# A linear attention followed by a Fourier mixing block: five output buffers, a smaller state mask, GpSimd operations one after the other, and a new order

## The chip, the cores and the metric

The kernel runs on one core of one Trainium2 chip. The metric is the time of one execution on the device, in microseconds (us), inputs and outputs in device memory. Five engines work side by side, each through its own queue in order: TensorE (PE in the profile: matmuls; PEld are its weight loads), VectorE (DVE), ScalarE (ACT), GpSimd (POOL) and SyncE (SP), which here issues DMAs only. ScalarE and GpSimd issue some DMAs too.

## The reference

Two blocks one behind the other. The first is a linear attention with a decaying state, over 4 batches, 8 heads, 768 steps and head size 48:

```python
for t in range(S):
    cur = np.einsum('bhd,bhe->bhde', u[None] * kt, vt)
    y[:, :, t] = np.einsum('bhd,bhde->bhe', rt, state + cur)
    state = w[None, :, :, None] * state + np.einsum('bhd,bhe->bhde', kt, vt)
```

The second takes the result as x (4 x 768 x 384), mixes it with the real part of a Fourier transform over both axes, normalizes, and adds an MLP of width 1536:

```python
X = np.fft.fft(np.fft.fft(x, axis=1), axis=2)
u = x + np.real(X)
un = (u - mean(u)) / np.sqrt(var(u) + 1e-06)
return u + np.maximum(un @ w_ch1, 0.0) @ w_ch2
```

## The kernel before

The sequence of a batch is cut into six chunks of 128 steps, 24 chunks in all. In a chunk k and r are scaled by powers of the decay (`KR`, line 386, with the tables `wtab`, lines 326 and 328, which ScalarE makes from `lw`, the logarithm of w), transposed (`tp` on TensorE at line 410, or a transposing DMA to `KRT`, line 416), multiplied with each other (`A`, line 444), masked (`MA`, on GpSimd at line 453 or VectorE at 456) and applied to v (`y`, line 535). The state is carried from chunk to chunk in `S` (line 490): the accumulated update is multiplied with a mask `WD` that is one, or the decay over three chunks, where a head's own block lies, and zero elsewhere. The result goes to `X` (line 543). Each batch is then folded by its symmetries (`EO`, `HH`, `XF`; the last is line 603, for the first batch 567), transformed over the sequence (`fp`, line 636) and over the width (`mp`, line 677), and gives the sum `UF` (line 689), scaled as `UB`, which is transposed to `UNT` on TensorE or by a DMA (line 747). The MLP takes half a batch at a time, eight halves of three blocks: `hp` (line 765, twelve groups of three matmuls), the relu `HT` (ScalarE at 770 or VectorE at 771), `mo` (line 786, four groups of three for each block), the epilogue `osb` (line 796, on VectorE) and the output DMA (line 799 from GpSimd, 800 from SyncE). `osb` h.j is block j of half h.

All operations are written down as a list of some 1,650 with names, alternatives (which engine does it, or nothing) and needs; the string `ORDER` is a list of their numbers with the alternative chosen, worked out by a planner beforehand. `emit` walks through it and issues each operation; an engine executes its operations in the order of this list. Many tiles live in rings of buffers; a new tile takes the buffer whose last user stands earliest in the list, and waits for that user. `osb` has a ring of three buffers. An operation waits for the data it needs, and for nothing else; two operations of GpSimd that share no data have no wait between them.

Matmuls on zeros (`idle`, line 272, of 512 columns, and line 366, of 384) can be put anywhere in the order; this one holds nine of the first kind and five of the second, all in the first 29 us.

The start (function `prelude`): ScalarE loads w, then a table set, computes `lw` (line 324), the six tables `wtab`, and after them `lwc` and `wdec` (lines 330 and 331), which need four small loads `wuc` that GpSimd issues (line 302). W1 comes in two halves and W2 in three parts, all issued by GpSimd (lines 840 and 843).

Of the kernel before, what the change touches and what calls it, by code (L numbers as in the profile page):

```python
# [61 lines left out]
class _Schedule:  # L62
# [12 lines left out]
    def emit(self, order):  # L75
        last = {}
# [5 lines left out]
        for k, (n, a) in enumerate(order):  # L82
# [7 lines left out]
            fn = o["alts"][a][2]  # L90
            if fn is not None:
                fn()
# [78 lines left out]
def kernel(  # L171
# [110 lines left out]
    def prelude():  # L282
# [30 lines left out]
        for i in range(2):  # L313
            op(("WD0", i), [("DVE", "msWD", lambda i=i: nc.vector.memset(WD[i], 0.0)),
                            ("POOL", "msWD", lambda i=i: nc.gpsimd.memset(WD[i], 0.0))], w=[("WD0", i)])
            one(("XF0", i), "DVE", "msXF", lambda i=i: nc.vector.memset(XFs[i][:, :, :, 4 * CH:], 0.0))
# [565 lines left out]
```

## Time and profile before

| | us |
|---|---|
| median of 3 runs | 182.74 |
| lowest and highest run | 179.83, 183.57 |
| profiled execution, span from the first to the last instruction | 180.9 |
| TensorE busy (share of the span) | 161.1 (89%) |
| VectorE | 133.4 (74%) |
| ScalarE | 109.8 (61%) |
| GpSimd | 84.1 (46%) |

The profiled execution gives its span alone, which lies 1.8 us under the median and inside the runs. Busy time is the time in which an engine executes something of the program; a busy TensorE may run at either of two clocks, and the granted clock is given as a share of the full one. Waits are put down to what ended them. A DMA's time to landing runs from its issue to the signal that its data have arrived.

### The profile page before, as it was taken

What the parts mean: (1) busy time and instruction counts of PE and PEld (TensorE: products, weight loads), DVE (VectorE), ACT (ScalarE), POOL (GpSimd) and SP (SyncE); (2) the same over time, 40 slices, a digit from 0 to 9 for tenths busy, and PEclk for the clock granted to TensorE, in tenths of its full rate; (3) what the DMA queues carried; (4) which work ended last, traced back from release to release, by engine and by line L of the source; (5) the groups of instructions that cost most, each with busy time, mean ns of one, the idle gap of its engine ahead of it and who ended that gap; (6) DMA issues with size and microseconds to landing.
All of it is one profiled execution on the core that took longest, in us unless ns stands there. A gap on an engine that the chain in (4) does not pass through costs nothing.

```text
span 180.9 us, 4262 instructions
## 1 busy us (share of the span) xinstructions
PE 161.1 (89%) x1595; PEld 112.7 (62%) x1595; DVE 133.4 (74%) x311; ACT 109.8 (61%) x264; POOL 84.1 (46%) x118
## 2 busy tenths in 40 slices
PE   6229987899799999999469999999999999999992
PEld 1126654887666766786236677756776866666661
DVE  5478899999699897999254688979859846542621
ACT  2366977398878987877332647888390553621430
POOL 6344857775563707498524233927783133101000
PEclk9999999699999999999957999999999999999999
DMA  6999999999488999969999995569510203711212
GB/s 125 202 219 211 242 203 201 225 183 198 76 151 178 156 210 184 243 150 180 137 264 224 213 203 119 145 127 210 114 35 2 80 11 65 196 49 43 87 43 87
DMA packets 98118, 27.08 MB, mean 150 GB/s; under 512 B 94369, under 2 KB 96930, under 8 KB 98098
## 3 DMA queue, kind: packets, MB, share of 16 engines
q1 hardware_dynamic: 92912, 21.70, 61.0%
q0 software_dynamic: 2064, 4.53, 11.4%
q10 hardware_dynamic: 3122, 0.59, 1.9%
q8 instruction: 12, 0.20, 0.5%
q14 instruction: 8, 0.07, 0.1%
HBM read 19.77 MB, written 4.72 MB: 135 GB/s over the span
## 4 chain that ended last, share of the span: by engine, by line
PE 72%; DVE 12%; DMA 9%; ACT 2%; issue 2%; SPq 1%; DVEq 0%; ACTq 0%
PE bank L765 27%; PE bank L786 25%; DMA out_dram<-osb 4%; PE bank L636 3%; PE bank L444 3%; PE bank L677 3%; DMA kr<-in_k_dram 3%; DVE KR L386 2%; DMA vt<-in_v_dram 2%; PE bank L410 2%; DVE MA L456 2%; PE bank L475 2%; PE bank L535 2%; DVE XF L567 2%; PE bank L514 1%
## 5 line engine op out<-in xcount | busy, mean ns | idle before, releaser
L765 PE MATMUL bank<-UNT,W 128*128 128x384 bf16 x288 | 56.5, 337 | 5.0 <-DVE osb L796 3.9
L786 PE MATMUL bank<-W,HT 128*128 128x384 bf16 x276 | 52.7, 326 | 0.0
L770 ACT ACTIVATE HT<-bank 128x384 bf16<-128x384 f32 x67 | 29.6, 497 | 31.7 <-PE bank L765 31.6
L765 PEld LDWEIGHTS <-W 128*128 128x128 bf16 x288 | 31.5, 116 | 19.5 <-issue 7.7
L786 PEld LDWEIGHTS <-HT 128*128 128x128 bf16 x276 | 25.9, 98 | 14.1
L453 POOL TENSOR_SCALAR_AFFINE_SELECT MA<-AC 128x512 bf16<-128x512 bf16 x26 | 17.1, 667 | 13.9 <-ACT AC L451 13.8
L796 DVE SCALAR_TENSOR_TENSOR osb<-bank,rstd,UF 128x384 f32<-128x384 f32 x23 | 14.1, 614 | 12.6 <-PE bank L786 8.1
L771 DVE TENSOR_SCALAR HT<-bank 128x384 bf16<-128x384 f32 x29 | 15.6, 551 | 8.4 <-PE bank L765 8.3
L386 POOL TENSOR_TENSOR KR<-kr,wtab 128x384 bf16<-128x384 f32 x17 | 17.3, 1030 | 5.7 <-ACT lwc L330 4.9
L410 PE MATMUL bank<-ident,KR 128*128 128x128 bf16 x112 | 12.5, 253 | 7.4 <-DVE KR L389 2.8
L386 DVE TENSOR_TENSOR KR<-kr,wtab 128x384 bf16<-128x384 f32 x25 | 16.4, 671 | 1.8 <-ACT wtab L326 1.8
L708 ACT ACTIVATE squares<-UF,sm 128x384 bf16<-128x384 f32 x24 | 14.8, 617 | 3.9 <-DVE UF L689 3.7
L451 ACT CAST AC<-bank 128x512 bf16<-128x512 f32 x26 | 14.8, 588 | 3.9 <-PE bank L444 2.1
L410 PEld LDWEIGHTS <-KR 128*128 128x128 bf16 x112 | 9.3, 114 | 11.5 <-DVE KR L386 4.1
L799 POOL DMA_DIRECT2D out_dram<-osb x11 | 6.3, 571 | 21.9 <-DVE osb L796 19.3
L456 DVE TENSOR_TENSOR MA<-bank,mtri 128x512 bf16<-128x512 f32 x22 | 14.7, 681 | 0.7 <-PE bank L444 0.6
L689 DVE SCALAR_TENSOR_TENSOR UF<-bank,X 128x384 f32<-128x384 f32 x21 | 11.1, 554 | 5.4 <-PE bank L677 4.7
L636 PE MATMUL bank<-te_t,XF 128*128 128x193 bf16 x108 | 13.0, 260 | 0.0
L523 DVE TENSOR_TENSOR TT<-V,bank 128x384 bf16<-128x384 bf16 x18 | 9.9, 547 | 2.2 <-ACT V L402 0.8
L636 PEld LDWEIGHTS <-XF 128*128 128x128 bf16 x120 | 10.8, 102 | 0.9
L644 ACT CAST TT<-bank 97x386 bf16<-97x386 f32 x13 | 7.1, 606 | 5.6 <-PE bank L636 5.5
L420 ACT COPY KRT<-bank 128x512 bf16<-128x512 bf16 x16 | 9.3, 592 | 1.5 <-PE bank L410 1.5
(109 smaller groups left out, 266.3 us busy)
## 6 DMA issues: line engine op xcount, KB each, us to landing
kr<-in_k_dram SPq DMA_DIRECT2D x23, 192.0 KB, 4.1
kr<-in_r_dram SPq DMA_DIRECT2D x23, 192.0 KB, 3.9
vt<-in_v_dram SPq DMA_DIRECT2D x23, 192.0 KB, 4.0
out_dram<-osb SPq DMA_DIRECT2D x12, 192.0 KB, 2.6
out_dram<-osb POOLq DMA_DIRECT2D x11, 192.0 KB, 3.3
W<-in_moe_w_ch_dram POOLq DMA_DIRECT2D x2, 576.0 KB, 9.0
W<-in_moe_w_ch_dram POOLq DMA_DIRECT2D x3, 384.0 KB, 6.4
te_t<-te_c SPq DMA_DIRECT2D x1, 579.0 KB, 5.7
```

What stands on the lines that cost most here:

```text
L386: eng.tensor_tensor(out=o, in0=x, in1=y, op=AluOp.mult)
L410: nc.tensor.transpose(tps[s]()[:, p, :], KR()[:, s, p, :], ident)
L451: op(("AC", i, a), [("ACT", "AC", lambda: nc.scalar.copy(AC(), A_ps[a]())), ("NONE", "", None)], r=[("A", i)], w=[("AC", i, a)], new=[AC], ...
L453: op(("MA", i, a), [("POOL", "MA", lambda: nc.gpsimd.affine_select(out=MA[a](), in_=AC(), pattern=[[0, NP], [1, 128]], base=0, channel_mul ...
L456: ("DVE", "MA", lambda: nc.vector.tensor_tensor(out=MA[a](), in0=A_ps[a](), in1=mtri.unsqueeze(1).to_broadcast([128, NP, 128]), op=AluOp.m ...
L636: nc.tensor.matmul(fp()[:, par, :], lhsT=lhsT[:, g * CH:g * CH + 128], rhs=rhs, start=(nb == 0 and par == 0), stop=(nb == last and par == ...
L708: ("ACT", "SQ", lambda: nc.scalar.activation(out=squares, in_=UF()[:, j, :], func=Act.Square, scale=-float(DM), bias=sm()[:, j:j + 1], acc ...
L765: nc.tensor.matmul(hp(), lhsT=W1[:, dt, ft // 4 * 512 + ft % 4:(ft // 4 + 1) * 512:4], rhs=UNT()[:, :, dt, :], start=(dt == 0), stop=(dt = ...
L770: op(("HT", hf, ft), [("ACT", "HT", lambda: nc.scalar.activation(out=HT()[:, ft, :], in_=hp(), func=Act.Relu, scale=-1.0)), ("DVE", "HT", ...
L771: ("DVE", "HT", lambda: nc.vector.tensor_scalar(out=HT()[:, ft, :], in0=hp(), scalar1=-1.0, scalar2=0.0, op0=AluOp.mult, op1=AluOp.max))],
L786: nc.tensor.matmul(mo(), lhsT=HT()[:, ft, j * 128:(j + 1) * 128], rhs=W2[:, ft, :], start=(ft == 0), stop=(ft == 11))
L796: one(("osb", hf, j), "DVE", "osb", lambda: nc.vector.scalar_tensor_tensor(out=osb(), in0=mo(), scalar=rstd()[:, j:j + 1], in1=UF()[:, j, ...
```

## The change

Four things change together.

1. `osb` has five buffers in its ring instead of three.
2. `WD`, the mask of the state, is kept as one number per row, pair and half (128 x 4 x 2) instead of being written out over the 48 columns; the state product reads it with a stride of zero. Its memsets and copies shrink with it.
3. `emit` adds a wait: every GpSimd operation that is not a DMA waits for the end of the GpSimd operation before it. After a DMA that GpSimd issues a nop is put in, and the next operation waits for that.
4. `ORDER` is new throughout: places, engines, and which tiles take which way. VectorE has 309 operations instead of 290, ScalarE 213 instead of 229 with its DMAs, GpSimd 122 instead of 114, TensorE 442 groups instead of 448. The nine zero matmuls of line 272 are left out; the five of line 366 stay. Two transposes on TensorE more stand for one transposing DMA less.

The diff, with the order cut to its ends:

```diff
-    def emit(self, order):
-        last = {}
+    def emit(self, tc, order):
+        nc, last, before = tc.nc, {}, None
...
-            fn = o["alts"][a][2]
-            if fn is not None:
-                fn()
+            eng, key, fn = o["alts"][a]
+            if fn is None:
+                continue
+            fn()
+            if eng != "POOL":
+                continue
+            if "dma" in key:
+                before = nc.gpsimd.nop().ins
+                continue
+            ins = next(i for i in reversed(nc.cur_bb.bb.instructions) if i.engine == mybir.EngineType.Pool)
+            if before is not None:
+                tc.add_manual_dep(ins, before.name, mybir.DependencyInfo(mybir.DependencyClass.Sync, mybir.DependencyReason.DATA),
+                                  reason="one after the other")
+            before = ins
...
 ORDER = """
-152 158 180.1 208 202 203 20 150 151 205 206 209 210 2 159 162 173 155 1 164 211 204 212 153 182 199.1 200.1 154 157
...
-1648.1 1652 1653 1654.1
+199 170.1 208 152 158 209 167.1 159 160 150 200 153 202 155 203 151 177 162 204 201.1 154 163 205 180.1 173 164 165
...
+1646 1647 1648.1
...
-    WD = [const([128, NP, 2, D], F32, f"WD{i}") for i in range(2)]
+    WD = [const([128, NP, 2], F32, f"WD{i}") for i in range(2)]
...
-    ring("osb", 3, [128, DM], F32)
+    ring("osb", 5, [128, DM], F32)
...
-            op(("WD0", i), [("DVE", "msWD", lambda i=i: nc.vector.memset(WD[i], 0.0)),
-                            ("POOL", "msWD", lambda i=i: nc.gpsimd.memset(WD[i], 0.0))], w=[("WD0", i)])
+            one(("WD0", i), "DVE", "tiny", lambda i=i: nc.vector.memset(WD[i], 0.0))
...
-            one(("WD", 0, a), "DVE", "ms192", lambda rows=rows, a=a: nc.vector.memset(WD[0][rows, :, a, :], 1.0), r=[("WD0", 0)])
-            one(("WD", 1, a), "DVE", "wdcopy", lambda rows=rows, a=a: nc.vector.tensor_copy(
-                WD[1][rows, :, a, :], wdec[rows, :].unsqueeze(2).to_broadcast([64, NP, D])), r=["wdec", ("WD0", 1)])
+            one(("WD", 0, a), "DVE", "tiny", lambda rows=rows, a=a: nc.vector.memset(WD[0][rows, :, a], 1.0), r=[("WD0", 0)])
+            one(("WD", 1, a), "DVE", "small", lambda rows=rows, a=a: nc.vector.tensor_copy(WD[1][rows, :, a], wdec[rows, :]),
+                r=["wdec", ("WD0", 1)])
...
-            op(("S", i + 1), [("DVE", "S", lambda: nc.vector.tensor_tensor(out=Sn(), in0=u_ps(), in1=d, op=AluOp.mult))]
+            op(("S", i + 1), [("DVE", "S", lambda: nc.vector.tensor_tensor(out=Sn(), in0=u_ps(), in1=d.unsqueeze(3).to_broadcast([128, NP, 2, D]), op=AluOp.mult))]
...
-        sch.emit(_order())
+        sch.emit(tc, _order())
```

Parts of the new order, read by their names, each in the sequence of its engine's queue:

```
GpSimd, start:   KR0.4 KR0.1 wuc.0.0 icol_i wuc.1.0 wuc.1.1 S0.2 wuc.0.1 ident ...
ScalarE, start:  load w, table set, load v of chunk 0, lwc, lw, six tables wtab, ...
GpSimd, end of the first batch's folds:  W1 (second half), HH 0.5.0, XF 0.5.0, MA 6.0, W1 (first half), KR 9.1, TR 0.0, ...
SyncE, batch 1:  KRT 16, KRT 17, UNT 1.0, k 19, r 19, output 0.1, UNT 1.1, v 17, KRT 14, ...
VectorE, batch 1:  MA 16.0, X 13, X 15, HT 2.7, HT 2.8, S 17, osb 1.2, HT 2.11, ...
TensorE, between the places of output 0.1 and osb 1.2:  hp 2.8, 2.5, 2.2, 2.11, 2.1, A 17, hp 2.6
```

In the old order GpSimd's outputs 0.1, 0.0, 1.1 and 0.2 stand among its arithmetic of batch 1, the output 1.1 right behind `TT` 15 and 16 places ahead of `osb` 1.2, which takes its buffer.

## Rows read from the trace of the kernel before

**Rows 1.** by stage (windows): stretch, busy us per engine (instructions), granted clock, DMA share, GB/s

```profile
13.10:47.90 34.80, 30.03 (x411) 22.96 (x411) 32.68 (x78) 27.14 (x65) 21.85 (x31) 0.95 1.04 203
47.90:70.00 22.10, 22.06 (x233) 15.27 (x234) 20.27 (x43) 18.75 (x46) 11.45 (x14) 1.00 0.88 160
...
84.00:90.00 6.00, 4.00 (x60) 2.81 (x58) 2.93 (x7) 3.19 (x8) 4.04 (x5) 1.00 1.17 143
90.00:98.00 8.00, 6.10 (x29) 3.21 (x29) 3.35 (x7) 1.64 (x4) 3.23 (x2) 0.57 1.09 244
98.00:177.60 79.60, 79.54 (x678) 55.54 (x676) 54.09 (x125) 43.44 (x111) 26.58 (x35) 1.00 0.45 104
```

**Rows 2.** VectorE's timeline: start us, us, line, operation, [idle before <- what ended it]

```profile
91.23 0.62 DVE L796 SCALAR_TENSOR_TENSOR osb<-bank,rstd,UF 128x384 f32<-128x384 f32 x1 [4.30 <-DMA out_dram<-osb]
```

**Rows 3.** chain that ended last, in order of time: start us, us, what

```profile
47.91 0.65 PE bank L765 x3
...
84.68 6.53 DMA out_dram<-osb
...
91.90 4.96 PE bank L765 x15
...
154.60 4.39 PE bank L765 x27
```

**Rows 4.** SyncE's DMA issues, 76 to 100 us (timeline, same columns)

```profile
78.12 4.05 SPq L416 DMA_TRANSPOSE KRT<-KR  x3
...
84.27 2.47 SPq L747 DMA_TRANSPOSE UNT<-UB  x1
```

**Rows 5.** by line: operation, tiles, shapes, count | busy us, mean ns | idle before

```profile
L523 DVE TENSOR_TENSOR TT<-V,bank 128x384 bf16<-128x384 bf16 x18 | 9.9, 547 | 2.2 <-ACT V L402 0.8 <-PE bank L508 0.7 <-ACT HT L770 0.7
...
L490 DVE TENSOR_TENSOR S<-bank,WD 128x384 bf16<-128x384 f32 x8 | 4.4, 548 | 0.0
...
L337 DVE COPY WD<-wdec 64x192 f32<-64x192 f32 x2 | 1.0, 484 | 0.0
...
L314 DVE MEMSET WD<- 128x384 f32 x2 | 0.8, 378 | 0.1
```

**Rows 6.** timeline of all engines, first 16 us

```profile
5.65 0.58 POOL L302 DMA_DIRECT2D wuc<-in_u_dram  x1
...
8.93 0.61 ACT L326 ACTIVATE wtab<-HT,ncol 128x384 f32<-128x384 f32 x1 [2.69 <-DMA kr<-in_k_dram]
...
10.96 0.19 ACT L330 ACTIVATE lwc<-wuc 128x4 f32<-128x4 f32 x1
```

**Rows 7.** DMA issues: tensors, queue, count, KB each, median us to landing

```profile
out_dram<-osb SPq DMA_DIRECT2D x12, 192.0 KB, 2.6
out_dram<-osb POOLq DMA_DIRECT2D x11, 192.0 KB, 3.3
W<-in_moe_w_ch_dram POOLq DMA_DIRECT2D x2, 576.0 KB, 9.0
...
wuc<-in_w_dram POOLq DMA_DIRECT2D x2, 0.8 KB, 4.2
```

**Rows 8.** GpSimd's timeline, 20 to 40 us

```profile
26.07 0.55 POOL L558 TENSOR_TENSOR HH<-X 128x192 bf16<-128x192 bf16 x1
26.58 0.56 POOL L567 TENSOR_TENSOR XF<-HH 128x196 bf16<-128x196 bf16 x1
...
33.77 1.39 POOL L558 TENSOR_TENSOR HH<-X 128x192 bf16<-128x192 bf16 x2
35.24 0.51 POOL L567 TENSOR_TENSOR XF<-HH 128x196 bf16<-128x196 bf16 x1
...
36.68 1.56 POOL L840 DMA_DIRECT2D W<-in_moe_w_ch_dram  x2
```

**Rows 9.** by line, the zero matmuls on TensorE

```profile
L272 PE MATMUL bank<-zero 128*128 128x512 bf16 x9 | 4.0, 512 | 1.5 <-DVE wuc L296 1.3 <-ACT KRT L420 0.2
...
L366 PE MATMUL bank<-zero 128*128 128x384 bf16 x5 | 1.8, 391 | 0.0
```

122 rows, old and new, of the table ORDER are left out of this document.

## The prediction

> **What bounds the kernel now.** I read four views: busy time by stage, the chain that ended last, the timeline of single engines, and the DMA issues. The stage table comes first [rows 1]. From 13.1 to 47.9 us VectorE (DVE) is busy 32.68 of 34.80 us: it prepares the first batch and sets the pace, and TensorE (PE) works beside it. From 47.9 us on, when the first matmul of the MLP starts, PE is busy 22.06 of 22.10, then 79.54 of 79.60 from 98 to 177.6. Those stretches are worth what their PE work is worth. In between lies the one hole: from 84 to 90 PE is busy 4.00 of 6.00, from 90 to 98 it is busy 6.10 of 8.00 at a mean granted clock of 0.57.
>
> The DVE timeline names the cause: the epilogue `osb` at 91.23 us waited 4.30 us for a DMA that was emptying its buffer [rows 2]. The chain shows the same, `out_dram<-osb` from 84.68 for 6.53 us, and behind it fifteen matmuls of L765 in 4.96 us, 0.331 each, where 27 of the same take 4.39 later, 0.163 each [rows 3]: PE came back at 1.2 instead of 2.4 GHz. That output had to wait on GpSimd's queue, and it travelled beside the transposing DMAs that SyncE issued from 78.12 and at 84.27 [rows 4]. By the rows the hole costs 2.00 + 1.90 idle and 6.10 x (1 - 0.57) = 2.6 of clock, 6.5 us in all.
>
> So the span reads: first MLP matmul at 47.9, then 177.6 - 47.9 = 129.7 us, of which 6.5 are the hole and 123.2 are PE work, then 3.3 us for the last epilogue and output: 47.9 + 123.2 + 6.5 + 3.3 = 180.9.
>
> **The change part by part.**
>
> *Five output buffers.* With three, `osb` 1.2 waits for the landing of output 1.1. With five, read off the new order by the same rule (the buffer whose last user stands earliest), it waits for output 0.1. That removes this wait, 6.5 us with its clock, if output 0.1 has landed. It is the third DMA on SyncE behind the transpose `UNT` 1.0, after k and r of chunk 19. Between its issue and `osb` 1.2 the new order puts six groups of three MLP matmuls on PE, 18 x 0.163 = 2.9 us. An output from SyncE lands after 2.6 us at the median [rows 7], at worst after the 6.53 of [rows 3]; so VectorE waits 0 to 3.6 us. PE has other banks to write meanwhile. I take 0.5 us of PE time and keep 0 to 3.6 (6.5 if the clock falls again, a rival below). `osb` 3.1 comes only 18 places after output 1.1, whose buffer it takes; VectorE is busy 54.09 of 79.60 us there [rows 1], and a wait of about 1 us hides in that idle time.
>
> *Mask as one number per row and head.* Two memsets of 378 ns become writes of a few numbers, and so do the two copies of 484 ns [rows 5]; 1.8 us in all, less some 0.3 for the short ones that stay. With the two memsets of ones beside them I take 1.8 off VectorE, all of it before the first MLP matmul. The state product now reads its second operand with stride zero. The product with a full operand takes 548 ns; the nearest row with a spread operand, `TT` at L523, takes 547 [rows 5]. I cost it at nothing; eight such products would have to grow by 60 ns each to cost half a microsecond.
>
> *The start.* In the new order ScalarE computes `lwc`, which needs all four small GpSimd loads `wuc`, before `lw` and the six tables of powers; in the old one it came after them, at 10.96 us [rows 6]. The last of the four was issued at 5.65 [rows 6]. It is now the eighth GpSimd operation, which I estimate at 4.3 us, and these loads land after 4.2 us [rows 7]: 8.5. `lw` and six tables follow, each about 0.5 apart, and the last table ends near 12.2. In the old order the tables were held as well, by ScalarE's own DMA issue, until 8.93, and ended at about 11 [rows 6]. So the late start of the first table is mostly absorbed: 0 to 1.1 us, and I take 0.8.
>
> *VectorE's queue.* Up to the last operation that the first MLP matmul needs, both orders put 95 operations on VectorE; the swaps are between operations of near length. The first batch therefore ends 0.8 - 1.8 = 1.0 us earlier for VectorE, at 46.9. But the second half of W1 is now issued behind three GpSimd operations that follow the last fold. The old order issued both halves from 36.68 [rows 8]; with the 0.8 of the start and one masking operation I put it at 38.2. These loads take 9.0 us to land [rows 7]: 47.2, and the third group of MLP matmuls needs them. I take 47.3 for the start of steady PE work, from 46.2 (only VectorE counts) to 48.5 (no gain, late W1).
>
> Until the last fold of batch 1 the new order has 146 VectorE operations where the old one has 138. Eight at the mean of that stretch, 20.27 / 43 = 0.47 us [rows 1], are 3.8 us. Against them stand VectorE's idle 22.10 - 20.27 = 1.8 us and 1.9 us by which the new order moves the first seq transform of that batch back on PE (three more groups of W2 matmuls, 9 x 0.163 = 1.5, and two transposes). That leaves 0.1; the bound without VectorE's idle time is 1.9. I take 0.3.
>
> *One GpSimd operation after the other.* Before, the next one started 0.04 us before the end of the last: 26.07 + 0.55 = 26.62 against 26.58. Where it waited for its predecessor's semaphore it started 0.08 after: 33.77 + 1.39 = 35.16 against 35.24 [rows 8]. So a wait costs 0.12 us where operations stand back to back. The first batch has 44 GpSimd operations up to its last `UB`: 5.3 us at most. GpSimd is idle 34.80 - 21.85 = 12.9 us from 13.1 to 47.9 [rows 1], and this covers it; cost 0, bound 5.3. Behind a waiting GpSimd operation stand its loads of W1 and W2 and its outputs; those have the 0.1 to 0.5 us that I gave W1. The early start in these rows is also what the Trainium skill says (GPSIMD Engine Reference, 2.1 Instruction dispatch): consecutive Pool instructions are no barrier for one another, and completion holds back only what waits for the semaphore; the trace agrees, by 0.04 us. By that rule the wait buys safety and no time, and the sum is the same.
>
> *PE's own list.* From the first MLP matmul on both orders hold the same operations, but for two more sets of four transposes in the new one: 0.4 us. The nine zero matmuls of 512 columns are gone [rows 9]; their effect on the clock is a rival.
>
> **Sum:** 47.3 + 123.2 + 0.4 + 0.3 + 0.5 + 3.3 = 175.0 us against the span of 180.9, a ratio of 0.967. The runs shown have a median of 182.74, 1.0% above this span (179.83 to 183.57), so I scale: 182.74 x 0.967 = 176.8.
>
> **The rivals.**
>
> *A. The wait moves to another output.* Output 0.1 stands behind a transposing DMA and two loads on SyncE, and the neighbours of [rows 4] are what made the old one slow. If it lands after 6.5 us and PE falls to 1.2 GHz again, the hole comes back whole: 175.0 - 0.5 + 6.5 = 181.0, times 1.01 is 182.8, no change. For it: VectorE takes its queue in order, so every other epilogue stands behind. Against it: six matmul groups of cover, and the output is issued by SyncE, not behind GpSimd's arithmetic.
>
> *B. TensorE stays slow in the first batch; slower than before.* The fourteen zero matmuls were 4.0 + 1.8 us of PE time, nine of them are left out [rows 9]. PE was busy 30.03 of 34.80 us at a mean clock of 0.95, 28.5 us at full clock; without the fillers of that stretch about 24. At 1.2 GHz this is 48 us, and from 13 us on the MLP would begin at 61: 61 + 124.4 + 3.3 = 188.7, times 1.01 is 190.6. It decides from a start of the MLP after 56.8 on. Against it: VectorE's list feeds PE as densely as before, and real work of two chunks now stands where fillers stood. The rule behind it is the Trainium skill's (TensorE: Matmul & The Clock Gate, Part 1: The HAM clock gate): "the default state is throttled, and activity releases the throttle". It speaks against leaving fillers out; [rows 3] agree in that PE came back slow from its idle time. By that rule alone the time would be that of B, by the rows' dense queue that of the sum.
>
> *C. The first batch pays for the GpSimd waits or the late tables.* With 5.3 us for the waits uncovered the MLP starts at 52.6: 52.6 + 124.4 + 3.3 = 180.3, scaled 182.1, within 2%. For it: many of these operations (KR, MA, XF) feed PE or VectorE directly. Against it: 12.9 us of idle time.
>
> **How the numbers follow.** Forecast 0.60, A 0.17, C 0.11, B 0.07, other losses that make it slower 0.05. About 2% is what a measurement of this kernel can tell from no change: 179.1 to 186.4. The forecast's own bounds: 46.2 without the two small losses gives 173.1, or 174.8 scaled; 48.5 with 1.9 and 3.6 would be 180.9 with all mishaps at once, so its own range is 173 to 180. With A and C the range is 172.5 to 184.5. Faster by over 2%: 0.60. Within 2%: A and C, 0.28. Slower: B and the rest, 0.12.
>
> **What would show it.** Right: the first L765 matmul between 46 and 48.5; no wait of `osb` for a DMA over 1 us between 80 and 95; PE busy without a hole and at clock 1.00 from there on; back-to-back GpSimd operations 0.08 us apart. Wrong: a stretch of clock below 0.6 after 50 us, a wait of PE for `osb` or `UNT` (A); a mean clock well under 0.95 before 48 us (B); GpSimd named as releaser in the first batch, or `lwc` much later than 8.5 (C).

## The result: half of what was forecast

The changed kernel takes 179.25 us (median of 20 runs, 178.33 to 181.37), the one before 182.14 (20 runs, 179.75 to 184.20). The ratio is 0.988 with an interval of 0.985 to 0.992: faster, but by less than 2%. The forecast was 176.8. The profiled execution has a span of 177.8 us against 180.9, where the sum gave 175.0. Ratios and the median spans below leave out executions over 1.5% above the fastest of the same kernel: 2 of 20 of the kernel after, 26 of the 64 of the kernel before that ran beside the experiments (median span 180.1 us instead of 180.7), 3 of the 10 of the run g4 described below (178.8 instead of 179.3).

The stages of the kernel after, cut as in [rows 1] (columns: busy time of each engine in the stretch, with its number of instructions; then the mean granted clock of TensorE, the DMA share and GB/s):

```profile
13.10:47.60 34.50, 29.15 (x410) 22.39 (x411) 32.36 (x79) 26.02 (x62) 24.09 (x32) 1.00 1.03 206
47.60:70.00 22.40, 22.26 (x230) 15.48 (x231) 20.50 (x44) 15.70 (x40) 15.48 (x21) 1.00 0.85 159
84.00:90.00 6.00, 6.00 (x63) 3.94 (x60) 5.66 (x13) 4.41 (x14) 4.42 (x6) 1.00 0.87 183
90.00:98.00 8.00, 7.60 (x73) 5.27 (x72) 6.31 (x12) 5.10 (x14) 4.99 (x7) 1.00 1.29 188
98.00:174.40 76.40, 75.40 (x661) 52.32 (x659) 56.58 (x133) 35.40 (x87) 26.80 (x36) 1.00 0.48 116
```

The hole of [rows 1] is gone: 6.00 of 6.00 and 7.60 of 8.00 us busy from 84 to 98, and the granted clock is 1.00, the level of 2.4 GHz, in every stage. Yet behind 98 us TensorE is idle for 1.00 us, where it was idle 0.06 before. The timeline of TensorE names every place where it waited after the first MLP matmul:

```profile
71.23 0.40 PE L420 MATMUL bank<-ident,KR 128*128 128x128 bf16 x4 [0.29 <-DVE KR L396]
94.56 0.25 PE L518 MATMUL bank<-UW,PR 128*128 128x2 bf16 x4 [0.40 <-POOL PR L442]
112.92 0.34 PE L687 MATMUL bank<-hid_t,TR 97*128 97x192 bf16 x2 [0.75 <-POOL TR L665]
120.21 2.60 PE L775 MATMUL bank<-UNT,W 128*128 128x384 bf16 x15 [0.23 <-DVE S L500]
```

In the kernel before, the same view had one such row, the hole. (The code stands ten lines lower after the change: L765 is now L775, L796 is L806, and so on.) The four idle times add to 1.67 us. By its own pace (the starts of its matmuls against the usual distance between the same two) TensorE falls behind by some 2.5 us, an estimate, since the matmul behind a wait also loses its overlap with the one ahead of it. From its first MLP matmul to its last matmul it took 126.75 us; the sum had 124.4.

Where two of the waits come from is seen in GpSimd's queue:

```profile
92.76 0.50 POOL L413 CAST V<-vt 128x384 bf16<-128x384 f32 x1 [3.92 <-DMA vt<-in_v_dram]
93.35 1.15 POOL L442 TENSOR_TENSOR PR<-KRT 128x512 bf16<-128x512 bf16 x1
...
111.46 0.58 POOL L809 DMA_DIRECT2D out_dram<-osb  x1
112.03 0.84 POOL L665 COPY TR<-TT 97x768 bf16<-97x768 bf16 x1
```

A cast of v waited 3.92 us for its load, and the product `PR`, which did not need it, stood behind. `TR` stood behind two products `KR` and the issue of an output.

### The profile page after: what moved, and what is told of

Read it like the earlier page. It is cut to its first block, busy times and chain, and to the rows that moved or that the text cites. A ratio compares the mean times of both kernels' runs of the same rounds, so it can differ in the third digit from the quotient of the medians.

```text
span 177.8 us, 4333 instructions
## 1 busy us (share of the span) xinstructions
PE 157.1 (88%) x1595; PEld 111.2 (63%) x1595; DVE 139.2 (78%) x330; ACT 102.5 (58%) x244; POOL 90.1 (51%) x126
## 2 busy tenths in 40 slices
DMA packets 97222, 26.82 MB, mean 151 GB/s; under 512 B 93313, under 2 KB 96130, under 8 KB 97202
## 3 DMA queue, kind: packets, MB, share of 16 engines
q0 software_dynamic: 1936, 4.13, 10.5%
## 4 chain that ended last, share of the span: by engine, by line
PE 64%; DVE 16%; ACT 7%; issue 5%; POOL 3%; DMA 2%; POOLq 0%; DVEq 0%; ACTq 0%
PE bank L775 23%; PE bank L796 21%; PE bank L646 4%; PE bank L687 4%; DVE KR L396 3%; PE bank L454 3%; DMA wuc<-in_w_dram 2%; DVE MA L466 2%; PE bank L545 2%; PE bank L485 2%; DVE TT L533 1%; PE bank L420 1%; DVE HH L604 1%; PE bank L524 1%; DVE HT L781 1%
## 5 line engine op out<-in xcount | busy, mean ns | idle before, releaser
L775 PE MATMUL bank<-UNT,W 128*128 128x384 bf16 x288 | 52.9, 327 | 0.5 <-ACT squares L718 0.3
L796 PE MATMUL bank<-W,HT 128*128 128x384 bf16 x276 | 51.7, 326 | 0.0
L775 PEld LDWEIGHTS <-W 128*128 128x128 bf16 x288 | 30.7, 114 | 12.9 <-issue 0.9
L780 ACT ACTIVATE HT<-bank 128x384 bf16<-128x384 f32 x58 | 26.2, 493 | 19.6 <-PE bank L775 19.5
L796 PEld LDWEIGHTS <-HT 128*128 128x128 bf16 x276 | 25.9, 98 | 14.5
L463 POOL TENSOR_SCALAR_AFFINE_SELECT MA<-AC 128x512 bf16<-128x512 bf16 x30 | 20.8, 693 | 15.4 <-ACT AC L461 12.8
L396 DVE TENSOR_TENSOR KR<-kr,wtab 128x384 bf16<-128x384 f32 x29 | 19.5, 690 | 6.3 <-ACT wtab L336 5.8
L781 DVE TENSOR_SCALAR HT<-bank 128x384 bf16<-128x384 f32 x38 | 20.1, 549 | 5.0 <-PE bank L775 5.0
L806 DVE SCALAR_TENSOR_TENSOR osb<-bank,rstd,UF 128x384 f32<-128x384 f32 x23 | 13.9, 611 | 7.3 <-PE bank L796 7.1
L413 POOL CAST V<-vt 128x384 bf16<-128x384 f32 x10 | 5.4, 537 | 15.8 <-DMA vt<-in_v_dram 15.5
L711 POOL TENSOR_SCALAR UB<-UF,sm 128x384 bf16<-128x384 f32 x13 | 7.9, 604 | 10.6 <-issue 5.5
L466 DVE TENSOR_TENSOR MA<-bank,mtri 128x512 bf16<-128x512 f32 x18 | 12.2, 681 | 0.2
L718 ACT ACTIVATE squares<-UF,sm 128x384 bf16<-128x384 f32 x18 | 11.1, 617 | 0.6 <-DVE UF L699 0.5
L454 PE MATMUL bank<-KRT 64*128 64x128 bf16 x192 | 10.4, 233 | 0.9 <-ACT KRT L430 0.9
```

The costliest lines, as they stand in the source:

```text
L396: eng.tensor_tensor(out=o, in0=x, in1=y, op=AluOp.mult)
L454: nc.tensor.matmul(A_ps[a]()[:, p, :], lhsT=KRT()[rows, 0, p, :], rhs=QT(p, rows), start=(p == 0), stop=(p == NP - 1), skip_group_check=True)
L463: op(("MA", i, a), [("POOL", "MA", lambda: nc.gpsimd.affine_select(out=MA[a](), in_=AC(), pattern=[[0, NP], [1, 128]], base=0, channel_mul ...
L466: ("DVE", "MA", lambda: nc.vector.tensor_tensor(out=MA[a](), in0=A_ps[a](), in1=mtri.unsqueeze(1).to_broadcast([128, NP, 128]), op=AluOp.m ...
L775: nc.tensor.matmul(hp(), lhsT=W1[:, dt, ft // 4 * 512 + ft % 4:(ft // 4 + 1) * 512:4], rhs=UNT()[:, :, dt, :], start=(dt == 0), stop=(dt = ...
L780: op(("HT", hf, ft), [("ACT", "HT", lambda: nc.scalar.activation(out=HT()[:, ft, :], in_=hp(), func=Act.Relu, scale=-1.0)), ("DVE", "HT", ...
```

## The experiments

The parts of the change were taken one by one, then work was added or taken away to see what the small waits hang on. In the table, the median in us is over all executions of a run and the span is the median over those kept; the last two columns are of the profiled one: the start of the first MLP matmul, and the time from there to TensorE's last matmul. The runs were measured in five rounds. In each of them the kernel before ran too; over all its executions its median span was 180.5 to 180.95 in every round, and over the 38 kept ones it is 180.1 (its profile: 47.91 and 129.63).

| run | what it is | median us | ratio to before, 95% | span | first MLP | to the end |
|---|---|---|---|---|---|---|
| after | the change | 179.25 | 0.988 [0.985, 0.992] | 177.30 | 47.62 | 126.75 |
| g4 | mask alone | 181.02 | 0.996 [0.988, 1.005] | 178.80 | 48.27 | 128.16 |
| e4 | mask, GpSimd waits | 180.84 | 0.992 [0.988, 0.996] | 179.15 | 48.36 | 128.90 |
| e2 | mask, five buffers | 178.83 | 0.978 [0.972, 0.984] | 177.15 | 47.59 | 126.31 |
| e3 | mask, five buffers, GpSimd waits | 180.03 | 0.983 [0.974, 0.992] | 177.70 | 48.47 | 125.90 |
| e1 | all but the GpSimd waits | 178.68 | 0.978 [0.973, 0.984] | 176.95 | 47.59 | 126.02 |
| f1 | after + 3.6 us of zeros | 184.18 | 1.013 [1.006, 1.019] | 182.45 | 48.02 | 130.64 |
| f2 | e2 + 3.6 us of zeros | 180.33 | 0.993 [0.988, 0.998] | 178.40 | 47.19 | 127.75 |
| f3 | after, light loads | 179.04 | 0.985 [0.977, 0.992] | 177.30 | 47.17 | 126.66 |
| f4 | e2, light loads | 175.28 | 0.963 [0.957, 0.969] | 173.60 | 46.57 | 123.44 |
| g1 | after, light VectorE | 179.36 | 0.983 [0.974, 0.993] | 177.65 | 47.59 | 126.65 |
| g2 | e2, light VectorE | 177.38 | 0.974 [0.965, 0.982] | 175.65 | 47.98 | 124.41 |
| g3 | after, eight HT to ScalarE | 179.14 | 0.983 [0.975, 0.991] | 177.30 | 47.40 | 126.32 |
| m1 | after, four places mended | 179.98 | 0.986 [0.975, 0.996] | 178.10 | 48.05 | 124.64 |
| m2 | e1, four places mended | 178.46 | 0.983 [0.979, 0.988] | 176.75 | 47.40 | 125.65 |
| h2 | g4, UNT 1.1 on TensorE | 180.73 | 0.996 [0.991, 1.000] | 179.00 | 47.99 | 127.52 |
| h4 | h2, three banks | 179.54 | 0.988 [0.979, 0.997] | 177.40 | 47.47 | 126.50 |
| h3 | e2, UNT 1.1 on TensorE | 178.69 | 0.982 [0.977, 0.987] | 176.95 | 47.61 | 125.90 |
| h5 | h3, three banks | 178.20 | 0.981 [0.976, 0.986] | 176.40 | 46.96 | 126.19 |

Executions of one kernel differ by 0.6 to 5 us, and many runs have four executions only. So a single profile is read for where the time goes and the medians for how much, and a few tenths of a us between two medians tell nothing.

### The parts of the change

e1 and e2 leave out the GpSimd waits:

```diff
-            if before is not None:
-                tc.add_manual_dep(ins, before.name, ...
+            if False:
+                tc.add_manual_dep(ins, before.name, ...
```

and likewise the nops. e2, e3, e4 and g4 put the old `ORDER` back; e4 and g4 also `ring("osb", 3, ...)`.

> The changed kernel with its new order, five buffers and small mask, but without the wait of each GpSimd operation for the one before it (and without the nops). Theory N (the new order itself gives back what the hole was worth, through denser queues on VectorE and GpSimd): no difference to the changed kernel, about 179 us, span 177 to 178.5, and small waits of TensorE after 47.6 us that sum to 2 to 3 us as there. Theory W (the GpSimd waits give it back): the small waits shrink below 1 us, span about 175.5, time about 177.

> The old order, with five output buffers and the small mask, no GpSimd waits. Theory H (the hole at 84 to 98 us was the wait of the epilogue for a buffer, and the old order has nothing else to lose): the hole is gone with its clock, 180.9 - 6.5 = 174.4 of span, perhaps 1 less for the small mask, about 175.5 us, ratio 0.96 to 0.97. Rival M (something else was late there, the transposing DMA for UNT, and the wait moves to it): 178 to 181 us, with TensorE waiting for UNT or at a granted clock under 0.8 between 84 and 98.

> The old order with five buffers, small mask and the GpSimd waits: the changed kernel but for the order. Theory N: as e2 within 0.5% (old order better than the new one by 2 to 3 us). Theory W: 1.5 to 3 us more than e2.

> The old order with three buffers, small mask, and the GpSimd waits: the kernel before plus the waits. Theory N: within 0.7% of before, about 182 us. Theory W: 1.5 to 3 us above before, 183.5 to 185, with the hole at 84 to 98 us still there in both.

> The kernel before with the small mask alone (old order, three buffers, no GpSimd waits). The prediction gave the mask 1.8 us of VectorE's time before the first MLP matmul and nothing behind it. If VectorE sets the start, the first MLP matmul comes at 46.9 or a little before, and the span at 180.0 with the hole still there; if the second half of W1 sets it, as e2 (47.59) suggests, 47.5 and a span of 180.5. Against e4 (first MLP matmul at 48.36) it shows what the GpSimd waits cost at the start: 0.8 us.

The mask alone (g4) has a ratio of 0.996 whose interval holds 1, and its first MLP matmul is no earlier than that of the kernel before. But e4, which has the mask and the GpSimd waits, is at 0.992 with an interval below 1, and the ten executions of each have nearly the same median (180.84 and 181.02 us, against 182.14 before). So about 1 us came with the smaller mask, behind the first MLP matmul; what made it is not shown. Two more buffers in the old order (g4 to e2) bring 1.65 us of span, 2.15 over all executions. The new order on top of it (e2 to e1) brings 0.2, which is nothing beside the scatter. The GpSimd waits cost 0.35, 0.55 and 0.35 us of span in the three pairs that differ by them alone (e1 to after, e2 to e3, g4 to e4); over all executions the same pairs give 0.6, 1.15 and -0.15, so this cost is not clear of the scatter.

So more than half of the gain is that of the buffers. They bring about 2 us in the medians, where the hole was worth 6.5 by the rows of the kernel before. In g4's profile it is worth 4.8 by the same sum: 3.40 idle, and 2.26 x 0.17 + 4.00 x 0.26 = 1.4 of clock (the timeline of TensorE, then two stretches as in [rows 1]).

```profile
91.74 4.13 PE L775 MATMUL bank<-UNT,W 128*128 128x384 bf16 x15 [3.40 <-DVE osb L806]
```

```profile
90.00:94.00 4.00, 2.26 (x10) 1.28 (x10) 2.61 (x5) 1.57 (x4) 0.18 (x1) 0.83 1.14 252
94.00:98.00 4.00, 4.00 (x33) 2.51 (x32) 1.85 (x4) 0.87 (x4) 3.06 (x2) 0.74 1.08 259
```

e2 shows what came in its place: its hole is gone too, and new waits have come, most of them for DMAs. The first of them, for a load of W2, lies ahead of the place of the hole, so the hole cannot have hidden it.

```profile
70.36 1.78 PE L796 MATMUL bank<-W,HT 128*128 128x384 bf16 x10 [0.72 <-DMA W<-in_moe_w_ch_dram]
90.98 0.68 PE L775 MATMUL bank<-UNT,W 128*128 128x384 bf16 x3 [0.42 <-DMA UNT<-UB]
112.69 0.25 PE L518 MATMUL bank<-UW,PR 128*128 128x2 bf16 x4 [0.66 <-POOL PR L442]
119.37 1.65 PE L775 MATMUL bank<-UNT,W 128*128 128x384 bf16 x9 [0.64 <-DMA UNT<-UB]
```

### Was the hole a lead for the others?

f1 and f2 put work where the hole was; f3 and f4 make the DMAs lighter.

```diff
 # f1, f2, in mlp1
+                for _ in range(22 if (hf, ft, dt) == (2, 0, 1) else 0):
+                    nc.tensor.matmul(hp(), lhsT=zero[:, 0:128], rhs=zero[:, 0:384], start=False, stop=False, ...)
 # f3, f4, in load
+            n = H if i < 8 else 1
-  ... out=dst(), in_=src[b, :, sl, :] ...
+  ... out=dst()[:, 0:n], in_=src[b, 0:n, sl, :] ...
```

> The new kernel with 22 matmuls of zeros (384 columns, 0.163 us each, 3.6 us of TensorE work in all) put into the accumulation of the hidden tile 0 of the third half batch, at about 86 us, where the kernel before had its hole. They add nothing to the result. Theory 'lead': the hole gave the other engines and the DMAs time to get ahead, and TensorE's small waits behind 86 us in the new kernel (0.56 at 94.6, 0.92 at 113.1, 0.39 at 120.2, 1.9 in all) are what is left when it is gone. Then 3.6 us more of work take their place: span 177.8 + 3.6 - 1.9 = 179.5, ratio to the new kernel 1.01. Rival 'fixed': these waits have nothing to do with the lead (a slow transfer, a neighbour on a queue), and the work is simply added: span 181.4, ratio to the new kernel 1.02, no faster than the kernel before.

> The old order with five buffers, the small mask and no GpSimd waits (e2), with the same 3.6 us of zero matmuls at about 87 us. In e2 TensorE waited behind that place 0.58 + 0.29 + 0.83 + 0.80 = 2.5 us. Theory 'lead': span 177.3 + 3.6 - 2.5 = 178.4. Rival 'fixed': 180.9, the span of the kernel before.

> The new kernel with the loads of k, r and v cut to one head of eight from chunk 8 on (the rest of each tile keeps an older chunk's numbers; the arithmetic is all done, on old data). It takes most of the DMA traffic of the MLP stretch away and leaves every instruction of the engines. Theory 'DMA': the small waits come from transfers that land late beside the loads (transposes, outputs, weights); without them the span falls to 177.8 - 2.0 = about 175.8 or below. Theory 'engines': in this order the waits name VectorE and GpSimd (KR, PR, TR), their queues are late whatever the DMAs do, and the span stays at 177.3 to 177.8.

> e2 (old order, five buffers, small mask, no GpSimd waits) with the same cut of the loads. Its waits name DMAs (a weight load 0.89 at 70.5, the transposes UNT 0.58 and 0.80) and GpSimd (0.83). Theory 'DMA': the first three go, span 177.3 - 2.3 = 175.0. Theory 'engines': the transposes are late because VectorE and GpSimd feed them late; span 176.8 to 177.3.

The two orders answer in opposite ways. In the old order 3.6 us of added work cost 1.25 us by the median spans (178.40 against 177.15), 1.9 by the means of all executions (10 and 4 of them) and 2.7 by the ratios of the table: less than was added by each of the three. The waits of e2 behind 87 us (0.42, 0.66 and 0.64) are gone, and one of 0.37 us is left.

```profile
69.84 1.79 PE L798 MATMUL bank<-W,HT 128*128 128x384 bf16 x10 [0.59 <-DMA W<-in_moe_w_ch_dram]
128.71 0.62 PE L454 MATMUL bank<-KRT 64*128 64x128 bf16 x16 [0.37 <-DMA KRT<-KR]
```

With light loads it runs 3.55 us shorter, and from the first MLP matmul on it takes 123.44 us. That is, within 0.3 us, the 123.2 of TensorE work that the prediction read from [rows 1]. So in the old order part of the hole, 0.9 to 2.35 us of the 3.6 put back, was a lead: while TensorE stood still, others caught up, and without the hole it meets them late. f4 tells that most of what is then lost hangs on the DMAs. It does not price the lead, for it also takes away the wait for W2 at 70.4 and any other late transfer.

In the new order neither holds. Light loads give nothing (177.30 both), and the added 3.6 us cost 5.15: TensorE waits at other places. Three of the five rows of f1 behind 87 us are for VectorE, whose `XF`, `osb` and `S` are made from TensorE's own earlier results; work added ahead of those gives no lead over them. That last step is argued from the code, not measured, and why the work cost more than its own length is not shown.

```profile
108.80 0.26 PE L646 MATMUL bank<-te_t,XF 128*128 128x193 bf16 x1 [0.78 <-DVE XF L613]
111.87 0.67 PE L646 MATMUL bank<-te_t,XF 128*128 128x193 bf16 x6 [0.48 <-DVE osb L808]
121.46 1.14 PE L775 MATMUL bank<-UNT,W 128*128 128x384 bf16 x6 [0.44 <-DMA UNT<-UB]
123.91 2.60 PE L775 MATMUL bank<-UNT,W 128*128 128x384 bf16 x15 [0.23 <-DVE S L500]
162.38 0.65 PE L775 MATMUL bank<-UNT,W 128*128 128x384 bf16 x3 [0.42 <-DMA UNT<-UB]
```

The Trainium skill (DMA: Bandwidth & Descriptors, Specifications) asks for 512 bytes or more per transfer if it is to go at line rate. In the profile page of after 93,313 of 97,222 packets lie under that; no run here changed the size of the packets, so what that costs in this kernel is not shown.

### What holds the new order back?

From 48 to 177 us the new order has VectorE busy longer than e2 has, and ScalarE shorter (first after, then e2):

```profile
48.00:177.00 129.00, 124.57 (x1170) 86.83 (x1168) 101.56 (x231) 70.00 (x172) 58.17 (x77) 1.00 0.63 135
```

```profile
48.00:177.00 129.00, 123.32 (x1162) 86.03 (x1160) 93.11 (x210) 77.20 (x191) 56.12 (x70) 1.00 0.72 137
```

g1 and g2 cut VectorE's work, g3 moves eight activations, m1 and m2 move four operations in the order:

```diff
 # g1, g2: PR, osb and UF on VectorE, fewer columns
+        n = NP if i < 8 else 1
+        co = DM if hf < 2 else 96
+            cu = 192 if b < 2 else 48
 # g3, in ORDER: HT 1.3, 1.5, 0.9, 2.7, 2.8, 2.11, 2.4, 3.4
-1362.1 ... 1366.1 ... 1332.1 ... 1412.1 ... 1414.1 ... 1420.1 ... 1406.1 ... 1448.1
+1362 ... 1366 ... 1332 ... 1412 ... 1414 ... 1420 ... 1406 ... 1448
 # m1, m2, in ORDER: V 17 behind PR 17; KR 18 and output 2.0 behind TR 2.1; KR 13 ahead of XF
-672 ... 710.1 ... 816.2 ... 822.1 ... 849.2 ... 1426 ... 1177.1
+710.1 672 ... 822.1 816.2 ... 1177.1 1426 849.2
```

> The new kernel with less work for VectorE behind the first MLP matmul: the products PR on VectorE keep one of four pairs from chunk 8 on, the folds UF a quarter of their columns from the third batch on, the epilogues osb a quarter from the second batch's outputs on (what is left out of the tiles keeps older numbers; nothing else changes). This takes about 10 us off VectorE between 48 and 178 us, a little more than the 8.5 us by which it is busier there in the new order (101.6) than in the old one (93.1). Theory 'VectorE': the new order loses to TensorE's waits what it moved to VectorE; the span falls from 177.8 to about 175.5. Rival 'round trips': the waits come from operations that stand too close behind their input in the order, or from GpSimd's queue; the span stays at 177.2 or above.

> e2 (old order, five buffers, small mask, no GpSimd waits) with the same cut of VectorE's work. Its waits went with the lighter loads (f4), so they are the DMAs': theory 'each order has its own limit' expects little, span 176.6 to 177.3. Rival: VectorE limits the old order as well; then the span falls by 2 us or more, to 175.3 or below.

> The new kernel with eight activations of hidden tiles (HT) between 54 and 100 us moved from VectorE to ScalarE, each at its place in the order; all work is done. VectorE 3.8 us less, ScalarE some 3.6 us more (8 x 0.45). Theory 'VectorE': span 1 us shorter, 176.8. Rival 'round trips': no change, or longer where ScalarE's queue is late now, 177.8 to 178.8.

> The new kernel with four places of its order changed, all work done: on GpSimd the cast of V 17 (which waited 3.92 us for its load) goes behind PR 17, and KR 18's second half and the issue of output 2.0 go behind TR 2.1; on VectorE KR 13's second half goes ahead of the transform XF that stood before it. Theory 'neighbours': TensorE's waits at 71.2 (0.3 to 0.5), 94.6 (0.4) and 112.9 (0.75) go: span 177.8 - 1.6 = 176.2. Rival 'path': TensorE waits at the next place instead, as it did with lighter loads (f3), span 177.2 to 177.8.

> m1 (new order, four places mended) without the GpSimd waits. m1's profiled execution had a span of 176.1, its others 178.1 to 178.8. Theory 'neighbours' with the waits' own cost (e1 against the new kernel: 0.8 us): 175.3 to 176.3 in the profile and a ratio of 0.97 to 0.975. Rival 'path': e1's number again, span 177.0, ratio 0.978.

The lighter VectorE did nothing for the new order (177.65), and g3 neither (177.30). g1 is a narrow test: of some 9 us that it takes off VectorE between 48 and 177, almost all lie behind 96 us, so it speaks only for the waits at 112.9 and 120.2, which stayed. In the old order the same cut, which takes 12 us off VectorE there, brought 1.5 us by the median spans (175.65): between the two expectations, and a hint that VectorE does its part there. The intervals of the ratios of e2 and g2 overlap, so it is no more than a hint.

m1's profiled execution did what 'neighbours' says. Of the four waits one is left, and the time to the end is 124.64 us, 2.1 us less than after's:

```profile
48.05 1.14 PE L775 MATMUL bank<-UNT,W 128*128 128x384 bf16 x6 [0.66 <-ACT X L555]
118.53 2.60 PE L775 MATMUL bank<-UNT,W 128*128 128x384 bf16 x15 [0.23 <-DVE S L500]
```

Its other executions were longer, 178.1, 178.4 and 178.8 us, and m2 gains 0.2 on e1 in the median. So single neighbours in GpSimd's and VectorE's queues made the waits seen in after's profile, but mending them is not shown to shorten the kernel. What keeps the new order at about 177 us in most executions stays open.

### What made the hole?

In g4 the hole is there as in the kernel before. h2 to h5 do the transposes of the second batch's second half (`UNT` 1.1) on TensorE instead of by a transposing DMA:

```diff
 # h2, h3, in ORDER: UNT 1.1
-1153.4 1155.4 1156.4 ... 1157.4 1159.4 ... 1158.4 ... 1154.4
+1153.2 1154.2 1155.2 1156.2 1157.2 1158.2 1159.2
 # h4, h5: five places earlier, transposes first
+1153.2 1155.2 1157.2 1154.2 1156.2 1158.2 1159.2
```

> Old order, three buffers, small mask, no GpSimd waits (g4, span 179.8, hole 3.56 us at 91.7 and 1.9 us of clock) with one transposing DMA less: UNT 1.1, issued at 84.5 and landed at 91.2 with an instruction fetch of 16 KB at 86.9 beside it, is done by nine transposes on TensorE (0.5 us) and three copies on ScalarE and VectorE. Theory 'stop': the DMA queues stood still for 1.5 us because a fetch met a transposing DMA; without one the outputs 1.0 and 1.1 land within 3.5 us of their issue instead of 4.5 to 6.5, the wait of osb falls under 1.5 us, the hole under 1 us, and the span to 176.0. Rival 'buffers': output 1.1 is late whatever travels beside it; the hole keeps 2.5 us or more, span 178.5 to 180.3.

> The same with five buffers (e2 with UNT 1.1 on TensorE). e2 waited 0.58 us at 91.0 for that transpose. Theory 'stop': the loads and outputs of 84 to 92 land 1 to 2 us earlier and the later waits shrink as they did with lighter loads: span 177.3 + 0.5 - 1.5 = 176.3. Rival: the later transposes meet their own fetches (104.3, 116.8) all the same, and the work on TensorE is added: 177.2 to 177.8.

> h2 (old order, three buffers, small mask, no GpSimd waits, UNT 1.1 on TensorE) with the three sets of transposes one place earlier in the order, where three different banks are free, ahead of the three copies. Theory 'stop': outputs 1.0 and 1.1 land in 3.4 to 4.4 us as in h2, osb waits about 1 us for output 1.1, TensorE has no hole over 0.5 us and stays at full clock: span 178.9 - 3.0 = 175.9 although three buffers stay. Rival 'buffers': TensorE, earlier by 1.7 us now, meets the wait for output 1.1 (1.5 us and more, and the clock): 178 or above.

> The same with five buffers (h3 with the transposes spread over three banks). In h3 TensorE's only waits after the first MLP matmul were the three for the bank, 1.66 us. Theory 'stop': they go and nothing comes in their place: span 176.9 - 1.5 = 175.4, ratio to the kernel before 0.965 to 0.97. Rival: the 1.66 us were a lead that hid other waits, as the zero matmuls of f2 did; span 176.5 to 177.3.

h2 made a wait of its own. All three sets of transposes took the one bank that was free, TensorE stood three times, and it came back at a granted clock of 0.57 from 86 to 90 us:

```profile
84.28 0.33 PE L731 MATMUL bank<-ident,UB 128*128 128x128 bf16 x3 [0.57 <-ACT UNT L737]
85.13 0.33 PE L731 MATMUL bank<-ident,UB 128*128 128x128 bf16 x3 [0.52 <-DVE UNT L738]
86.02 0.34 PE L518 MATMUL bank<-UW,PR 128*128 128x2 bf16 x8 [0.57 <-ACT UNT L737]
```

h4, with three banks, has no such wait for the bank: against g4 the hole shrinks from 3.40 to 1.29 us, the clock stays at 1.00, and the span goes from 178.80 to 177.40 although three buffers stay.

```profile
90.92 2.60 PE L775 MATMUL bank<-UNT,W 128*128 128x384 bf16 x15 [1.29 <-DVE osb L806]
```

That is between the two expectations (175.9 and 178), and the intervals of the two ratios overlap. The two outputs that GpSimd issues there, which by the order are 1.1 and 0.2 (the expectations call them 1.0 and 1.1), landed after 5.05 and 4.85 us instead of 6.03 and 5.29. So beside the transposing DMA an output took up to 1 us longer. But that is not what made the hole so short. Counted from the first MLP matmul, output 1.1, for which `osb` 1.2 waits, landed at the same time in both (42.8 us), and TensorE came to the hole 2.1 us later in h4, which has nine transposes and three small waits (0.33, 0.40 and 0.25) more ahead of it. What h4 gains is the clock: the fifteen matmuls behind the hole take 2.60 us in it, 4.13 in g4.

With five buffers (h5) no wait for an output is left and the span is 176.40, 0.75 less than e2, by median spans the shortest that leaves nothing out; its ratio, 0.981 [0.976, 0.986], is not apart from e1's and e2's. So the missing buffers made the hole (g4 and e2 differ by nothing else). That the transposing DMA beside the output made it longer is likely from the landing times, but h4 does not show it, since TensorE came to the hole later there.

## Why the prediction was half right

*The bound now.* Right behind 48 us: one hole, made by `osb` waiting for an output. g4 has it, e2 has not, and two buffers are all that differs. Ahead of it, VectorE did not set the start of the MLP: in the kernel before, the last tile `UNT` that the first MLP matmul reads was ready at 46.79, the second load of W1 landed at 47.78, and the matmul began at 47.91. In all runs of the old order it began 0.14 us behind that landing.

*The start.* Right in size: 47.62 us against 47.3. `lwc` came at 8.18 (8.5 forecast), the last table ended at 11.95 (12.2). The second load of W1 was issued at 38.95 (38.2) and landed 8.6 us later, at 47.53, 0.09 us ahead of the first MLP matmul. So not only the third group waited for it, as the prediction has it, but already the first; in e2 the wait is put down to this load:

```profile
47.59 0.65 PE L775 MATMUL bank<-UNT,W 128*128 128x384 bf16 x3 [0.90 <-DMA W<-in_moe_w_ch_dram]
```

So the 1.0 us that the smaller mask should save VectorE ahead of the MLP went nowhere (g4).

*The mask.* Right that the spread operand is free: the state product takes 552 ns against 546 (medians). The prediction had nothing for the mask behind the first MLP matmul; g4 and e4 have about 1 us there, unexplained.

*The GpSimd waits.* The price of one is right: 36.85 + 0.76 = 37.61, and the next operation starts at 37.69, 0.08 later.

```profile
36.85 0.76 POOL L568 TENSOR_TENSOR HH<-X 128x192 bf16<-128x192 bf16 x1
37.69 0.51 POOL L577 TENSOR_TENSOR XF<-HH 128x196 bf16<-128x196 bf16 x1
```

Their sum was put at nothing; by the kept medians it is 0.35 to 0.55 us, which is within the scatter.

*The buffers.* The step that failed. The sum took the hole's 2.00 + 1.90 + 2.6 = 6.5 us as given back whole, 123.2 + 0.4 + 0.3 + 0.5 = 124.4 for the rest of the kernel, and 126.75 were measured. The mechanism was right (`osb` waited for no DMA in the kernel after, the clock was 1.00); the term was too large, because the stretch behind the hole was read as worth its TensorE work whatever came ahead of it. [rows 1] show it without idle time, but behind a stop of 3.9 us. In the old order f2 measures what that stop had been paying for: of 3.6 us put back, 0.9 to 2.35 come out again. With light loads 6.2 us of the 6.5 are to be had (129.63 to 123.44), so there the loss hangs on the DMAs. In the new order, the one that was forecast, something of the same size was lost (126.75 against 124.4), at small waits for GpSimd and VectorE and not to the DMAs (f3); f1 finds no lead there, and the cause stays open.

The size of the hole was also read from one execution, and one with more of it than most. The mean granted clock of that execution was 0.972. Of the 64 executions of the kernel before that ran beside the experiments, 14 had 0.972 or less (median span 181.55 us) and 32 had 0.990 or more (the 28 of these at 0.990 and 0.991: 180.2). One per cent of the 161.1 us that TensorE is busy is 1.6 us, so by this estimate half of the executions did not have 2.6 us of lost clock to give back.

The trace of before held a hint. The transpose issued at 78.12 [rows 4] landed at 81.42 and TensorE used it at 81.71; the next two landed at 82.75 and 84.15 and were used at 82.97 and 84.43. Margins of 0.2 to 0.3 us, ahead of the hole, hint that TensorE ran just behind its transfers.

*The rivals.* A did not come: the wait did not move to another output. B did not come: TensorE's granted clock was 1.00 from 13.1 us on in the profiled execution, so the nine zero matmuls were not needed for it. C did not come as such: the start was on time. What came was not among them: several waits of 0.2 to 0.75 us at unconnected places. The marks set for 'right' (no wait of `osb`, clock 1.00, no hole, 0.08 us) were all met by a kernel that gained half; they looked for one large stop and would have had to ask for the sum of small ones.

## What to carry to other kernels

Before a stall of the busiest engine is counted as a gain, ask by how much each later transfer and each other engine's result came ahead of its use, and how much of that lead was made by the stall itself: a stretch that looks full behind a stall may be full because of it. The cheap test is to put as much harmless work where the stall was, once it is removed; what it does not cost was never to be gained. It finds a lead where there is one (f2); where it finds none (f1), the gain can be missing all the same. And a stall that differs from execution to execution is priced from several of them, not from one profile. A change in the order of in-order queues is best read by what stands behind each operation that waits for a load or issues a DMA.

## What was not expected of the hardware

A transposing DMA and an instruction fetch in flight together stopped nearly all DMA traffic for a while. In g4, UNT 1.1 was under way from 84.53 to 91.23 and a fetch of 16 KB began at 86.9. From 86 to 90 us the DMA view shows (40 slices of 0.1 us; queue q8 is the fetch):

```profile
DMA  9999999969991231993000020009094998994992
GB/s 242 265 222 227 241 232 251 230 102 358 143 159 13 44 46 41 97 69 46 0 0 0 0 49 0 3 31 36 20 74 102 266 136 236 236 243 62 177 497 51
DMA packets 1659, 0.52 MB, mean 131 GB/s; under 512 B 1628, under 2 KB 1628, under 8 KB 1658
```

In h4 the same stretch has the same fetch, at 86.4, and no transposing DMA:

```profile
DMA  9999988999899997998978999999979634456779
GB/s 213 240 234 257 379 171 171 175 188 200 169 292 317 373 432 246 357 352 158 261 169 171 186 196 204 380 288 326 444 225 388 231 127 177 125 127 140 184 154 196
DMA packets 3071, 0.96 MB, mean 241 GB/s; under 512 B 2976, under 2 KB 2976, under 8 KB 3069
```

The traffic falls under 100 GB/s for 1.8 us in the first and never in the second. It is the same in the other traces of the old order: the eight that do `UNT` 1.1 by DMA have 1.3 to 1.8 us on end under 100 GB/s behind that fetch, and h2 to h5, where no transposing DMA is under way, have at most 0.5 in the 2.5 us behind it.

Over all traces of this case, 48 transposing DMAs behind 46 us had a fetch of 16 KB begin within 3 us of their issue, and landed after 4.47 us at the median; the 220 others after 3.24, nine in ten of them within 4.2. It is no full account: the transposes at 59 to 61 us in the old order took 5.6 to 8.3 us, beside the loads of W2, with a fetch only in their last 2.3 us or none at all. h2 to h5 removed one such meeting, and the transposes issued at 99 to 101 and 113 to 116 us met their own fetches all the same.
